# Priority of the first-stage matmuls over x's second half, and a split of the last output stores, in an S4D + gated-GLU kernel

## Chip, core and metric

The kernel runs on one core of a Trainium2 chip. The metric is the device time of one execution in microseconds (us); the median of 3 runs of the kernel before is 713.99 us (711.97 to 716.0). Engines: PE is TensorE, DVE VectorE, ACT ScalarE, POOL GpSimd, SP SyncE.

## What is computed

With `xn` the layer norm of `x` (2048 positions, D = 448 channels), the result is `x + S4D(xn) + GLU(xn)`. The first branch is a long convolution with a kernel generated from 256 complex modes per channel, the second a gated MLP with F = 1792:

```python
# S4D branch: K from exp(A dt pos), then a convolution by FFT
P = jnp.exp((A * dt[:, None])[:, :, None] * pos[None, None, :])
K = 2.0 * jnp.einsum("dn,dnl->dl", C, P).real
y = irfft(rfft(u_t, 2 * L) * rfft(K, 2 * L)[None], 2 * L)[:, :, :L]
y = y + u * D_skip
# GLU branch
h = sigmoid(xn @ w_gate) * (xn @ w_up)
h @ w_down
```

All of it is float32 in accuracy: a float32 operand of the GLU is split into a high and a low part (`hh`/`hl`, `wh`/`wl`, `dh`/`dl`, `xh`/`xl`), and three products of the parts are summed.

## The kernel before

Two Python generators run side by side and hand their instructions to a scheduler: `conv()` for the S4D branch and `glu()` for the MLP. A table of estimated weights decides which generator gets the next turn; the scheduler then orders each engine's instructions by a rank (their place in the program, lowered by `HP` = 300 inside `with hp(HP):`) and by what it holds to be ready. On the chip each engine runs its own list strictly in that order, so an instruction that waits holds up all that stands behind it.

The GLU runs in two halves of 1024 positions. In each half `gate` (L695) multiplies x's transposed blocks by a 128-wide slice of the gate and up weights (L709, 11 matmuls per PSUM bank `gu`), ACT takes the tanh (`th`, L717), DVE multiplies (`hf`, L720), ACT and DVE split the product (`hh` L725, `hl` L727), and the down projection (`po`, L825) adds into `acc` by a DVE instruction (L830). `th`, `hf`, `hh`, `hl`, `acc` all have the raised rank.

The convolution first generates its kernel: per group of 8 channels two matmuls `tr` (L542), four ACT instructions `S` (L548 to L551), POOL products `me` and `mf` (L520), three large DVE products `Et`, `Et`, `Ft` (L602 to L604), and 32 small matmuls `ko` (L616) of 128 rows by 32 columns of PE. Later, in `spectra`, the two spectra are multiplied and turned back (L902, L929, L962), and DVE adds the result to the accumulators (L970).

In the last group of the GLU's first half (`cross`), the second half of x is prepared in four pairs of blocks (8, 10, 12, 14). `pair_norm` normalizes two blocks, `pair_turn` transposes them (L213, with copies L219 to L226), and `pair_first` (L681) does the first stage of their Fourier transform: four groups g, each two matmuls (L280) of 32 rows by 64 columns of PE into one `gu` bank, a copy of that bank to SBUF by ACT (L689) and a store to `x1_d` by ACT's queue (L691). The pool of `gu` banks has four buffers, shared by `gate`, `po`, `pair_turn` and `pair_first`: a matmul into a new bank waits until the bank's last reader is done.

At the end of the program the last group writes the output. `out` (L235) issues four stores, one for each 32 partitions, dealt round a list of queues. `accs[2]` holds blocks 8 to 11, `accs[3]` blocks 12 to 15. The first channel half (0 to 223) of the convolution is added long before the end; the second (224 to 447) is added by the four DVE instructions L970 that stand between the down projections of blocks 14 and 15.

Of the kernel before, what the change touches and what calls it, by code (L numbers as in the profile page):

```python
# [20 lines left out]
D = 448  # L21
# [15 lines left out]
HP = 300  # L37
Y0 = (8, 1)
CP = D // 4
H = D // 2  # L40
# [91 lines left out]
def s4d_glu_kernel(ctx, tc, io):  # L132
    nc = tc.nc
    hp = tc.high_priority
# [56 lines left out]
    def acc_tile():  # L191
        return pg.tile([128, 4, D], F32, name="acc", bufs=2)
# [37 lines left out]
    accs = [acc_tile() for _ in range(2)]  # L230

    def blocks(t, g, b0, nb):
        return t[g, :, b0 // 8, b0 // 4 % 2, b0 % 4 : b0 % 4 + nb]

    def out(src, b0, nb, ds, engs):  # L235

        for g in range(4):
            eng = engs[g % len(engs)]
            eng.dma_start(blocks(out_t, g, b0, nb)[:, :, ds], src[32 * g : 32 * g + 32, b0 % 4 : b0 % 4 + nb, ds])
# [33 lines left out]
    def row(b, g):  # L273
        return 32 * (b // 4 % 2) + 8 * g + 4 * (b // 8) + b % 4

    def x_first_stage(to, xn, g):

        s = slice(32 * g, 32 * g + 32)
        for i in range(2):
            nc.tensor.matmul(to[64 * i : 64 * i + 64], wx[s], xn[i][s], start=True, stop=True)  # L280
# [400 lines left out]
    def pair_first(b, xns):  # L681

        x1 = pg.tile([128, 2, D], F32, name="x1", tag="wraw", bufs=1)
        pss = [psg.tile([128, 512], F32, name="gu", bufs=4) for _ in range(4)]
        for g in range(4):
            x_first_stage(pss[g][:, :D], xns, g)
        for g in range(4):
            to = x1[:, g] if g < 2 else pg.tile([128, D], F32, name="x1", tag="rd", bufs=RB)
            nc.scalar.copy(to, pss[g][:, :D])  # L689
            r = row(b, g)  # L690
            nc.scalar.dma_start(  # L691
                x1_d[:, r : r + 2].rearrange("h i k d -> (i k) h d"), to.rearrange("p (h d) -> p h d", h=2)
            )
# [36 lines left out]
    def glu():  # L730
        for half in range(2):
# [4 lines left out]
            for fs_ in ORDER[half]:  # L736
# [3 lines left out]
                final = half == 1 and fs_ is ORDER[1][-1]  # L740
# [4 lines left out]
                if cross:  # L745
                    xts = {b: pair_load(b) for b in range(8, 16, 2)}
                    step = lambda f_, b: f_(b, xts[b])
                    mid = [(pair_norm, 8), None, (pair_first, 8), (pair_first, 10)]
                    end = [(), ((pair_turn, 8), (pair_norm, 10)), ((pair_turn, 10), (pair_norm, 12)), ((pair_turn, 12), (pair_norm, 14))]
                    downs = {(0, 0): (pair_first, 12), (0, 1): (pair_turn, 14), (0, 3): (pair_first, 14)}  # L750
# [54 lines left out]
                for t in range(2):  # L805
                    acc = accs[2 * half + t]
                    for b in range(4):
                        if final and (t, b) == (0, 1):

                            yield None  # L810
                        if final and t == 1 and b >= 2:

                            sp_mm[:] = glu_mm
                            for m in (4 * b - 8, 4 * b - 6):
                                lasts[0](1, m)
                            if b == 3:
                                out(accs[2], 8, 4, slice(H, D), (nc.sync, nc.scalar))
                                out(accs[3], 12, 3, slice(0, D), (nc.sync, nc.scalar))
                        po = psg.tile([128, D], F32, name="po", tag="gu", bufs=4)
                        bs = slice(128 * b, 128 * b + 128)  # L820
                        n = 0
                        with tc.issue_after(sp_mm[0].ins) if glu_on else nullcontext():
                            for (hh, hl), (dh, dl) in zip(hs[t], wts):
                                for a_, w_ in ((hh, dh), (hh, dl), (hl, dh)):
                                    glu_mm[:] = [nc.tensor.matmul(  # L825
                                        po, a_[:, bs], w_, start=(n == 0), stop=(n == 3 * fc - 1)
                                    )]
                                    n += 1
                        with hp(HP):
                            v.scalar_tensor_tensor(  # L830
                                acc[:, b], po, 0.5, acc[:, b], ALU.mult, ALU.add
                            )
                        yield 0.6 * fc
                        if cross and (t, b) in downs:
                            step(*downs[t, b])
                    if cross:
                        nc.sync.dma_start(acc_d[:, 4 * t : 4 * t + 4], acc)
                    if final and t == 0:
                        out(acc, 8, 4, slice(0, H), (nc.gpsimd,))
                    elif final:  # L840
                        out(acc, 15, 1, slice(0, D), (nc.sync, nc.scalar))

    def spectra(pf):

# [265 lines left out]
    xq, psc, raws, acl, marks, slots, pqs = list(x_first), [], [], [], [None, None], {}, []  # L1110
    W1s, GGs, act, exps = [], [], [], []
    gens = [conv(), glu()]
    total = [sum(Y0) + 11 * WP + 8 * WX + 34 + NCK * WK + HOLE + 17 * WS, 2 * (4 + NFT * 14.8) - HELD]
    done = [0.0, 0.0]
# [40 lines left out]
```

## Time and profile before

| What | Value |
|---|---|
| median of 3 runs | 713.99 us |
| time of the profiled execution | 710.54 us |
| its span, first to last instruction | 708.8 us |
| busy PE / DVE / ACT / POOL | 94% / 78% / 60% / 54% of the span |
| mean granted TensorE clock | 0.988 |

The profiled execution is 3.45 us below the median, inside the spread of the runs. In the views, "idle" in square brackets is the time an engine waited just before the instruction and the name behind the arrow is what ended the wait. A count x8 in the trace's rows of L280 is 4 of the program's matmuls, and x64 of L616 is 32: each of these float32 matmuls leaves two records.

### The profile page before, as it was taken

How to read it: one execution, taken by the hardware profiler on the slowest of the kernel's cores; microseconds unless marked ns; L12 is line 12 of the kernel's file. 1: busy time of each engine (PE TensorE's matmuls, PEld its weight loads, DVE VectorE, ACT ScalarE, POOL GpSimd, SP SyncE). 2: the span in 40 equal slices, each digit the busy share in tenths (PEclk: the TensorE clock that was granted, in tenths of full speed). 3: DMA queues.
4: the chain of work that ended last, by engine and by line, in shares of the span. 5: the costliest groups of instructions: out<-in, count | busy, mean ns of one | idle time of the engine just before them, and what ended most of it. 6: DMA issues, size and time to landing. Idle time of an engine off the chain costs nothing. (4 is left out here: it accounts for less than half of the span.)

```text
span 708.8 us, 19098 instructions
## 1 busy us (share of the span) xinstructions
PE 668.1 (94%) x7752; PEld 523.7 (74%) x7752; DVE 555.7 (78%) x766; ACT 428.7 (60%) x678; POOL 384.9 (54%) x433
## 2 busy tenths in 40 slices
PE   2798999999999998999999999999999999999996
PEld 2575878878877875756878878877777777777784
DVE  5899987699899998898478899988946555566544
ACT  3656965578689779877577788778543322322320
POOL 2101227655999999777446698798765001344001
PEclk9999999999999998989999999999999999999999
DMA  9956274554253544546833333242269988999756
GB/s 200 239 149 204 70 230 150 170 183 132 63 169 135 169 123 135 162 146 202 258 112 103 92 112 108 68 138 82 54 179 280 257 236 238 266 272 221 182 146 182
DMA packets 93031, 117.22 MB, mean 165 GB/s; under 512 B 12240, under 2 KB 76624, under 8 KB 92944
## 3 DMA queue, kind: packets, MB, share of 16 engines
q1 hardware_dynamic: 65376, 91.75, 46.3%
q10 hardware_dynamic: 24896, 18.13, 8.7%
q0 software_dynamic: 2672, 6.13, 3.2%
q8 instruction: 61, 1.00, 0.6%
q14 instruction: 26, 0.21, 0.1%
HBM read 72.13 MB, written 43.84 MB: 164 GB/s over the span
## 5 line engine op out<-in xcount | busy, mean ns | idle before, releaser
L520 POOL TENSOR_TENSOR me<-me,pm 128x32 f32<-128x32 f32 (+1 forms) x168 | 154.9, 922 | 66.8 <-DVE Et L603 38.1
L520 POOL TENSOR_TENSOR mf<-mf,pm 128x64 f32<-128x64 f32 (+1 forms) x112 | 116.9, 1044 | 5.1
L709 PE MATMUL gu<-xh,wh 128*128 128x512 f32 x336 | 100.1, 405 | 3.8 <-DVE acc L830 1.6
L709 PE MATMUL gu<-xh,wl 128*128 128x512 f32 x336 | 96.9, 393 | 0.0
L709 PE MATMUL gu<-xl,wh 128*128 128x512 f32 x336 | 95.1, 390 | 0.0
L602 DVE TENSOR_TENSOR Et<-me,S 128x1024 f32<-128x1024 f32 x56 | 80.2, 1433 | 11.6 <-ACT S L551 10.3
L825 PE MATMUL po<-dh,hh 128*128 128x448 f32 x224 | 84.2, 376 | 3.1 <-ACT hh L725 1.9
L548 ACT ACTIVATE S<-tr 128x1024 f32<-128x1024 f32 x56 | 57.7, 1030 | 44.9 <-PE tr L542 41.0
L604 DVE TENSOR_TENSOR Ft<-mf,S 128x1024 f32<-128x1024 f32 x56 | 80.1, 1431 | 5.3 <-PE ko L616 3.7
L603 DVE TENSOR_TENSOR Et<-me,S 128x1024 f32<-128x1024 f32 x56 | 80.4, 1436 | 4.8 <-ACT me L533 4.5
L825 PE MATMUL po<-dh,hl 128*128 128x448 f32 x224 | 82.4, 369 | 0.3 <-DVE hl L727 0.3
L825 PE MATMUL po<-dl,hh 128*128 128x448 f32 x224 | 82.3, 368 | 0.0
L709 PEld LDWEIGHTS gu<-xh,wh 128*128 128x128 f32 x336 | 60.8, 189 | 24.2 <-issue 4.4
L709 PEld LDWEIGHTS gu<-xh,wl 128*128 128x128 f32 x336 | 63.4, 189 | 14.7 <-DVE ve L255 0.7
L709 PEld LDWEIGHTS gu<-xl,wh 128*128 128x128 f32 x336 | 63.0, 188 | 13.5
L725 ACT CAST hh<-hf 128x512 fp32r<-128x512 f32 x56 | 34.9, 623 | 62.4 <-DVE hf L720 61.4
L616 PEld LDWEIGHTS ko<-Et,Ft 128*32 128x32 f32 x3584 | 54.7, 112 | 24.2 <-issue 13.4
L720 DVE SCALAR_TENSOR_TENSOR hf<-th,gu 128x512 f32<-128x512 f32 x56 | 38.1, 680 | 39.9 <-PE gu L709 35.2
L786 POOL TENSOR_TENSOR dl<-rd,dh 128x448 fp32r<-128x448 f32 x14 | 25.6, 1830 | 78.8 <-ACT dh L785 68.5
L616 PE MATMUL ko<-Et,Ft 128*32 128x64 f32 x3584 | 65.2, 223 | 2.6 <-DVE Ft L604 2.4
L551 ACT ACTIVATE S<-S,hpi 128x1024 f32<-128x1024 f32 x56 | 65.5, 1170 | 0.0
L717 ACT ACTIVATE th<-gu 128x512 f32<-128x512 f32 x56 | 33.5, 599 | 49.4 <-PE gu L709 43.0
(208 smaller groups left out, 1318.0 us busy)
## 6 DMA issues: line engine op xcount, KB each, us to landing
sk_d<-sk ACTq DMA_DIRECT2D x14, 512.0 KB
sx<-x_d SPq DMA_DIRECT2D x32, 224.0 KB
skl<-sk_d SPq DMA_DIRECT2D x16, 448.0 KB
vp<-v_d SPq DMA_DIRECT2D x16, 448.0 KB
v_d<-vt SPq DMA_DIRECT2D x14, 448.0 KB
ph<-ph_d SPq DMA_DIRECT2D x224, 24.0 KB
wt_d<-wh SPq DMA_DIRECT2D x9, 512.0 KB
wt_d<-wl SPq DMA_DIRECT2D x9, 512.0 KB
```

What stands on the lines that cost most here:

```text
L520: ins = nc.gpsimd.tensor_tensor(m[:, :, w + a : 2 * w : n], m[:, :, a:w:n], par(base + i).unsqueeze(2).to_broadcast([128, 4 * DC, w // n]) ...
L548: nc.scalar.activation(rows(cs), pv, AF.Abs)
L551: sins[:] = [nc.scalar.activation(cs, cs, AF.Sin, scale=-TWO_PI, bias=hpi)]
L602: v.tensor_tensor(Et[:, :, :, 32:64], two(me[:, :, 32:64]), S[:, 1::-1], ALU.mult)
L603: v.tensor_tensor(Et[:, :, :, 0:32], two(me[:, :, 0:32]), S[:, 1:3, :, ::-1], ALU.mult)
L604: fts[:] = [v.tensor_tensor(Ft, two(mf), S[:, 3:5], ALU.mult)]
L616: mm = nc.tensor.matmul(ko[32 * j : 32 * j + 32, sl], Ft[:, cc, DC * h + 4 * q + j], Et[:, cc, DC * h + 4 * q + j], start=(k == 0), stop=( ...
L709: glu_mm[:] = [nc.tensor.matmul(ps, a_, b_, start=(n == 0), stop=(n == len(mm) - 1))]
L717: marks[0] = nc.scalar.activation(th, pgu[0], AF.Tanh, scale=0.5)
L720: marks[1] = v.scalar_tensor_tensor(hf, th, 1.0, pgu[1], ALU.add, ALU.mult)
L725: nc.scalar.copy(hh, hf)
L825: glu_mm[:] = [nc.tensor.matmul(po, a_[:, bs], w_, start=(n == 0), stop=(n == 3 * fc - 1))]
```

## The change

Two edits. First, `pair_first` wraps its matmuls (through `x_first_stage`, L276) and ACT's copies in `hp(HP)`, so that both have the rank of the gate's functions; its DMA issues keep theirs. Second, the output stores of blocks 12 to 15 are cut in another way. Before: blocks 12 to 14 whole after the last L970, block 15 whole after its L830. After: of blocks 12 and 13 the first channel half is stored by POOL's queue as soon as block 13's L830 is done, the second half by SP and ACT after L970; blocks 14 and 15 go together, whole, after block 15's L830.

```diff
@@ pair_first
-        for g in range(4):
-            x_first_stage(pss[g][:, :D], xns, g)
+        with hp(HP):
+            for g in range(4):
+                x_first_stage(pss[g][:, :D], xns, g)
         for g in range(4):
             to = x1[:, g] if g < 2 else pg.tile([128, D], F32, name="x1", tag="rd", bufs=RB)
-            nc.scalar.copy(to, pss[g][:, :D])
+            with hp(HP):
+                nc.scalar.copy(to, pss[g][:, :D])
@@ glu, final group, second half of its positions
                                 out(accs[2], 8, 4, slice(H, D), (nc.sync, nc.scalar))
-                                out(accs[3], 12, 3, slice(0, D), (nc.sync, nc.scalar))
+                                out(accs[3], 12, 2, slice(H, D), (nc.sync, nc.scalar))
...
+                        if final and (t, b) == (1, 1):
+                            out(acc, 12, 2, slice(0, H), (nc.gpsimd,))
...
                     elif final:
-                        out(acc, 15, 1, slice(0, D), (nc.sync, nc.scalar))
+                        out(acc, 14, 2, slice(0, D), (nc.sync, nc.scalar))
```

Lines 687 to 816 of the kernel before stand two lower in the changed one, those behind 832 four lower. The instructions outside the stretch of the four pairs and the tail keep their order but for single steps.

**PE, pair 10.** Here `gu<-xt,wx` are `pair_first`'s matmuls (two rows' worth, x2, is one group g), `ko<-Et,Ft` the convolution's small matmuls, `gu<-ident,xt` transposes, `tr` the convolution's phase matmuls. Before:

```order
L709 MATMUL gu<-xl,wh 128x512 x3
L280 MATMUL gu<-xt,wx 64x448 x4
L213 MATMUL gu<-ident,xt 64x128 x2
L542 MATMUL tr<-sel,ph_1111 128x512 x2
L616 MATMUL ko<-Et_1104,Ft 32x64 x32
L280 MATMUL gu<-xt,wx 64x448 x4
L709 MATMUL gu<-xh,wh 128x512 x3
```

The same place on PE in the changed kernel:

```order
L711 MATMUL gu<-xl,wh 128x512 x3
L280 MATMUL gu<-xt,wx 64x448 x2
L616 MATMUL ko<-Et_1104,Ft 32x64 x11
L280 MATMUL gu<-xt,wx 64x448
L213 MATMUL gu<-ident,xt 64x128 x2
L280 MATMUL gu<-xt,wx 64x448
L616 MATMUL ko<-Et_1104,Ft 32x64 x17
L280 MATMUL gu<-xt,wx 64x448 x2
L616 MATMUL ko<-Et_1104,Ft 32x64 x4
L542 MATMUL tr<-sel,ph_1111 128x512 x2
L280 MATMUL gu<-xt,wx 64x448 x2
L711 MATMUL gu<-xh,wh 128x512 x3
```

The eight matmuls stood in two runs of four; now they stand in five runs, two of them of a single matmul, with pieces of one `ko` group between them.

**DVE, pair 12.** The row `hf<-th,gu` is the GLU product that frees the bank for `pair_first`'s first group; `Et`, `Et`, `Ft` are the convolution's large products; `xl` are the splits of the transposed blocks. Before:

```order
L602 TENSOR_TENSOR Et_1104<-me_1109,S_1103 128x32x32
L603 TENSOR_TENSOR Et_1104<-me_1109,S_1103 128x32x32
L720 SCALAR_TENSOR_TENSOR hf<-th,gu 128x512
L269 TENSOR_SCALAR xt<-xt,ys,zs 128x448
L220 TENSOR_TENSOR xl<-gu,xh 128x2x256
L604 TENSOR_TENSOR Ft<-mf_1108,S_1103 128x1024
```

DVE at the same place in the changed kernel:

```order
L722 SCALAR_TENSOR_TENSOR hf<-th,gu 128x512
L269 TENSOR_SCALAR xt<-xt,ys,zs 128x448
L602 TENSOR_TENSOR Et_1104<-me_1109,S_1103 128x32x32
L603 TENSOR_TENSOR Et_1104<-me_1109,S_1103 128x32x32
L729 TENSOR_TENSOR hl<-hf,hh 128x512
L604 TENSOR_TENSOR Ft<-mf_1108,S_1103 128x1024
```

`hf` has moved ahead of two `Et` products, and `xl` (no longer in the six rows) behind `Ft`.

**SP, the last stores.** `ac` holds blocks 0 to 7, `acc` the accumulators of blocks 8 to 15. Before:

```order
L945 DMA v_d<-vt 128x896
L951 DMA vp<-v_d 16x32x224
L239 DMA out_dram<-ac 32x4x224 x4
L239 DMA out_dram<-acc 32x4x224 x2
L239 DMA out_dram<-acc 32x1344 x2
L239 DMA out_dram<-acc 32x448 x2
```

The end of SP's list in the changed kernel:

```order
L949 DMA v_d<-vt 128x896
L955 DMA vp<-v_d 16x32x224
L239 DMA out_dram<-ac 32x4x224 x4
L239 DMA out_dram<-acc 32x2x224 x2
L239 DMA out_dram<-acc 32x4x224 x2
L239 DMA out_dram<-acc 32x896 x2
```

ACT's list ends in the same way. The small stores of blocks 12 and 13 (32x2x224) now stand ahead of those of blocks 8 to 11, and the last ones are twice as large (32x896 for 32x448). POOL's list gains four stores 32x2x224 at its end.

## The prediction

> **What bounds the kernel now.** I read the busy table in stretches of 20 us first, then the same table in stretches of 5 us around the four pairs, PE's waits there, and the timeline. Columns: length, busy time and instruction count of PE, PE's weight loads, DVE, ACT and POOL, then the granted clock, the DMA share, GB/s.
>
> ```profile
> 60.00:80.00 20.00, 17.21 (x83) 14.96 (x84) 19.31 (x38) 17.39 (x38) 0.00 (x0) 1.00 0.50 148
> ...
> 360.00:380.00 20.00, 19.87 (x266) 16.14 (x265) 16.18 (x19) 14.36 (x22) 12.97 (x19) 1.00 0.44 143
> ...
> 460.00:480.00 20.00, 19.76 (x323) 16.00 (x322) 17.51 (x15) 14.88 (x22) 19.69 (x20) 1.00 0.52 155
> ...
> 680.00:700.00 20.00, 20.00 (x223) 16.23 (x219) 10.68 (x21) 1.50 (x3) 2.18 (x4) 1.00 0.54 138
> ```
>
> PE is full from 340 us on: 19.87 and 19.76 of 20 in two stretches of the middle, 20.00 at the end. What delays PE at the pairs should therefore reach the end of the program nearly one to one. The pairs themselves look different:
>
> ```profile
> 275.00:280.00 5.00, 3.75 (x74) 1.53 (x62) 5.00 (x6) 5.00 (x9) 4.92 (x4) 0.93 0.15 49
> 280.00:285.00 5.00, 5.00 (x73) 3.15 (x73) 3.38 (x3) 5.00 (x9) 4.84 (x7) 0.50 0.56 177
> 285.00:290.00 5.00, 5.00 (x79) 3.79 (x77) 2.90 (x5) 3.24 (x6) 3.83 (x6) 0.89 0.47 142
> 290.00:295.00 5.00, 4.97 (x92) 3.43 (x85) 5.00 (x7) 4.85 (x9) 2.12 (x4) 1.00 0.73 225
> 295.00:300.00 5.00, 5.00 (x92) 3.03 (x85) 4.94 (x5) 5.00 (x10) 4.84 (x4) 1.00 0.39 119
> ...
> 305.00:310.00 5.00, 3.27 (x37) 1.26 (x38) 5.00 (x9) 5.00 (x9) 4.60 (x8) 1.00 0.29 101
> 310.00:315.00 5.00, 5.00 (x53) 2.91 (x53) 4.96 (x6) 5.00 (x9) 4.69 (x5) 0.50 0.42 128
> 315.00:320.00 5.00, 5.00 (x71) 3.83 (x70) 4.65 (x6) 3.83 (x7) 0.27 (x2) 0.82 0.27 92
> ...
> sum 75.00, PE 69.61 PEld 46.34 DVE 63.80 ACT 64.66 POOL 59.66; mean PE 4.64 PEld 3.09 DVE 4.25 ACT 4.31 POOL 3.98
> ```
>
> Two things are to be seen. From 265 to 340 us PE is idle 75 - 69.61 = 5.4 us, while DVE has 63.80 of 75 filled, so PE and DVE bound this part by turns. And twice, behind a thin stretch (3.75 and 3.27 of 5), the clock is halved: work lost is (0.07 + 0.50 + 0.11) x 5 = 3.4 us the first time, (0.50 + 0.18) x 5 = 3.4 us the second.
>
> **The first edit: pieces.** What a run of L280 costs PE is in its timeline (start, length, count):
>
> ```profile
> 275.76 0.97 PE L280 MATMUL gu<-xt,wx 32*64 32x448 f32 x4
> 277.98 0.97 PE L280 MATMUL gu<-xt,wx 32*64 32x448 f32 x4 [1.25 <-DVE xl L220]
> 278.88 0.41 PE L213 MATMUL gu<-ident,xt 128*64 128x128 f32 x2
> ...
> 294.60 0.98 PE L280 MATMUL gu<-xt,wx 32*64 32x448 f32 x8
> 295.51 0.41 PE L213 MATMUL gu<-ident,xt 128*64 128x128 f32 x2
> ...
> 305.91 1.99 PE L280 MATMUL gu<-xt,wx 32*64 32x448 f32 x8 [0.92 <-DVE hf L720]
> ...
> 322.36 0.99 PE L280 MATMUL gu<-xt,wx 32*64 32x448 f32 x12
> ...
> 326.18 0.41 PE L213 MATMUL gu<-ident,xt 128*64 128x128 f32 x2 [0.75 <-DVE xl L223]
> ```
>
> Four records (one group g) hold PE for 278.88 - 277.98 = 0.90 us, eight (two groups) for 295.51 - 294.60 = 0.91, twelve for 0.99. The groups lie in different rows of the array and run side by side, but only when they follow each other. The price is per run, not per matmul. Before, the trace has 4 runs in pair 8 (each group by itself), 2 in pair 10, 3 in pair 12 (the row of 1.99 us is two that a wait parts) and 2 in pair 14: 11. The changed order has 5, 5, 3 and 4: 17. Six more runs are 6 x 0.90 = 5.4 us of PE. Four of the runs are single matmuls, for which the trace has no row; between half a run (0.45) and a whole one, I take the whole, since both matmuls of a group already lie side by side in different columns. The lower end is 5.4 - 4 x 0.45 = 3.6 us. Ten cuts of `ko` for seven add a few tenths at most, which I leave out.
>
> What of this shows, pair by pair:
>
> - Pair 8, one run more, and six of the 32 `ko` matmuls moved behind the 1.25 us gap, all just as the clock halves: up to 2 us. But DVE waits behind it now:
>
> ```profile
> DVE hf L720 <- PE gu L709: 2.1, 1, 2.1
> ...
> DVE Ft L604 <- PE ko L616: 1.6, 1, 1.6
> ```
>
> The changed order lets DVE do an `Et` ahead of that `hf`, so the 2.1 us are used and little is left of the delay. I take +0.2, bounds 0 and +2.
> - Pair 10, three runs more: PE has no gap from 290 to 300 us that could take them. +2.7, lower bound 3 x 0.90 - 2 x 0.45 = +1.8.
> - Pair 12, no run more. `hf` ran late because two `Et` stood ahead of it on DVE:
>
> ```profile
> 303.18 2.08 DVE L603 TENSOR_TENSOR Et<-me,S 128x1024 f32<-128x1024 f32 x1
> 305.18 0.67 DVE L720 SCALAR_TENSOR_TENSOR hf<-th,gu 128x512 f32<-128x512 f32 x1
> ```
>
> Now it stands ahead of them and PE's gap of 0.92 us goes: -0.9. Next late is `xl`, which moves behind `Ft` (bound: a new gap of one `Et`, about +2).
> - Pair 14, two runs more, +1.8, with gaps of 0.75 and 0.17 us beside them that can take half: +0.9, bounds 0 and +1.8. Here a down projection comes to wait for DVE's last split of the earlier pair, which stands behind five large products.
>
> Sum +2.9 us. ACT's copies only change places; its queue of small DMA issues is off the path, since x1_d is read much later.
>
> **The clock.** Everything ahead of the first halved stretch is unchanged, so that one stays. The second followed a thin stretch made of L280 runs and two gaps. The changed order fills that place better, but thins out pair 10 (4.5 us of L280 runs in about 6.5 us, each on a quarter of the array or less) and pair 14. I keep the count at two: 0, bounds -3.4 and +6.8. [...]
>
> **The second edit: the tail.**
>
> ```profile
> 694.75 0.62 DVE L830 SCALAR_TENSOR_TENSOR acc<-po,acc 128x448 f32<-128x448 f32 x1 [1.23 <-PE po L825]
> ...
> 699.41 2.21 DVE L970 TENSOR_TENSOR acc<-acc,pv 128x448 f32<-128x448 f32 x4 [0.34 <-PE pv L962]
> 702.12 0.62 DVE L830 SCALAR_TENSOR_TENSOR acc<-po,acc 128x448 f32<-128x448 f32 x1 [0.50 <-PE po L825]
> ```
>
> ```profile
> 703.81 1.79 SPq L239 DMA_DIRECT2D out_dram<-acc  x2
> ```
>
> ```profile
> DMA  9999679977899899999989998894794000000000
> GB/s 315 275 359 287 187 215 343 319 231 203 207 203 191 207 291 347 410 379 362 311 287 311 335 335 263 263 287 128 263 343 136 8 0 0 0 0 0 0 0 0
> DMA packets 1677, 1.93 MB, mean 215 GB/s; under 512 B 287, under 2 KB 1549, under 8 KB 1677
> ```
>
> The last rows cover 700 to 709 us in 40 slices: the DMA engines are nearly full until slice 31, 700 + 31 x 0.225 = 707.0, moving 1.93 MB in 7 us, 276 GB/s. The last data is ready at 702.12 + 0.62 = 702.74, but SP issues its store at 703.81 only: the tail is bound by bytes. The change takes 4 x 56 KB = 0.23 MB out of it, 0.23 / 0.276 = 0.83 us, and has POOL issue them from 694.75 + 0.62 = 695.4 on, into a hole:
>
> ```profile
> DMA  8677596200030000000004988988999999767997
> ```
>
> (694 to 702 us, 0.2 us each: almost nothing from 695.6 to 698.2.) Against it, the last four stores carry 0.46 MB instead of 0.23. If they leave no earlier than now, they end 0.83 us later. They should leave earlier, because what stands ahead of them is smaller and can start with the second L970 instruction. I take -0.6, bounds -0.8 and +0.8.
>
> **Sum.** +2.9 + 0 - 0.6 = +2.3 us: the profiled execution of 710.54 us becomes 712.8, and the median of 713.99 becomes **716.3 us** (+0.3%).
>
> **Rivals.**
>
> - *A further halved stretch.* Pair 10, cut into single runs, falls under what the clock needs, around 300 us, or pair 14 does around 318 us. For it speaks that both halved stretches follow such places; against it that 325 to 330 us was left at 1.00. Price 3.4 us: 716.3 + 3.4 = 719.7, slower. It decides if pair 10's 5 us hold more L280 than other work on PE. Two of them: 723.
> - *One halved stretch less.* `hf` ahead of the `Et` products closes the gaps at 305 and 309 us, the clock stays, and no other place is thin enough: 716.3 - 3.4 = 712.9.
> - *DVE sets the pace.* PE's extra runs lie under DVE's work altogether (63.80 of 75 us), so +2.9 becomes -0.9, and the second halved stretch goes as well: 713.99 - 0.9 - 3.4 - 0.6 = 709.1, faster. Against it speaks pair 10, where PE had no gap.
> - *Only the tail counts*: pieces and gaps cancel, 713.4.
>
> **Chances.** Forecast 0.42; further halved stretch 0.23; one less 0.14; DVE sets the pace 0.15; only the tail 0.06. Faster by over 0.5% (below 710.4, about what a measurement can tell from no change) is the DVE case and a little of its neighbour: 0.18. Slower by over 0.5% (above 717.6) is the further stretch and some 0.4 of the forecast, whose bounds reach 2 us up: 0.39. Within: 0.43. The range leaves out the DVE case's lower half and two further stretches: 710.0 to 721.5.
>
> **What would show it.** In the changed profile: runs of x2 or x4 of L280 at 0.9 us each, 17 of them; PE still full around 295 us, with pair 10's gate matmuls 2 to 3 us later than at 298; no wait of L280 for `hf` in pair 12; two stretches at clock 0.50; DMA at the end done about 4.3 us behind the last L830 + 0.62, now 707.0 - 702.7. Wrong would be: single runs at 0.45 us or less, a third stretch at 0.50 or only one, or a delay at 340 us that is gone at 540.

## The result and the profile after

The change makes the kernel **slower by 0.7%**: 717.25 us median (714.32 to 722.64, 10 runs) against 712.52 us (710.1 to 716.0, 10 runs) of the kernel before on the same chip, ratio 1.0069, 95% interval 1.0043 to 1.0096, so 3.1 to 6.8 us. The predicted 716.3 us lies 0.95 us below, inside the range, but the predicted difference was 2.3 us and the measured one is 4.7. That the times lie so close is in part luck: the 713.99 us from which the forecast started, a median of three runs, stands 1.47 us above the median of ten. The profiled execution of the changed kernel is the fastest of its ten: 714.32 us, span 712.5, mean clock 0.989 (before: 710.54, 708.8, 0.988). Ratios are taken without runs that lie over 1.5% above the fastest of their kernel; for one experiment (`turns_up_tail`) that leaves out three of twelve, and its median stands higher than its ratio says.

Where the time came in, the start of one and the same `hf` product on DVE tells, behind the four pairs and near the end. In the timeline of the changed kernel:

```profile
343.95 0.69 DVE L722 SCALAR_TENSOR_TENSOR hf<-th,gu 128x512 f32<-128x512 f32 x1 [4.46 <-PE gu L711]
...
681.18 0.69 DVE L722 SCALAR_TENSOR_TENSOR hf<-th,gu 128x512 f32<-128x512 f32 x1 [3.05 <-PE gu L711]
```

The same two in the kernel before:

```profile
340.31 0.69 DVE L720 SCALAR_TENSOR_TENSOR hf<-th,gu 128x512 f32<-128x512 f32 x1 [4.41 <-PE gu L709]
...
676.70 0.69 DVE L720 SCALAR_TENSOR_TENSOR hf<-th,gu 128x512 f32<-128x512 f32 x1 [3.05 <-PE gu L709]
```

3.64 us late behind the pairs, 4.48 us at 677 us, and 712.5 - 708.8 = 3.7 at the end: the delay is made at the pairs, grows a little, and the tail gives 0.8 back. Now pair 8 on PE in the changed kernel (start, length, idle time ahead):

```profile
273.66 0.97 PE L280 MATMUL gu<-xt,wx 32*64 32x448 f32 x4 [0.76 <-DVE hf L722]
...
275.12 0.97 PE L280 MATMUL gu<-xt,wx 32*64 32x448 f32 x4
...
277.81 1.75 PE L280 MATMUL gu<-xt,wx 32*64 32x448 f32 x2 [1.16 <-DVE xl L220]
279.49 0.64 PE L213 MATMUL gu<-ident,xt 128*64 128x128 f32 x2
280.06 1.75 PE L280 MATMUL gu<-xt,wx 32*64 32x448 f32 x2
...
283.46 1.76 PE L280 MATMUL gu<-xt,wx 32*64 32x448 f32 x4
285.15 1.94 PE L616 MATMUL ko<-Et,Ft 128*32 128x64 f32 x64
```

Five runs, three of them at half clock at 1.7 us each (285.15 - 283.46). And pair 10, at full clock:

```profile
296.85 0.97 PE L280 MATMUL gu<-xt,wx 32*64 32x448 f32 x4
297.75 0.54 PE L616 MATMUL ko<-Et,Ft 128*32 128x64 f32 x22
298.22 0.96 PE L280 MATMUL gu<-xt,wx 32*64 32x448 f32 x2
299.11 0.41 PE L213 MATMUL gu<-ident,xt 128*64 128x128 f32 x2
299.44 0.96 PE L280 MATMUL gu<-xt,wx 32*64 32x448 f32 x2
300.34 0.75 PE L616 MATMUL ko<-Et,Ft 128*32 128x64 f32 x34
```

A single matmul (x2 records) holds PE for 299.11 - 298.22 = 0.89 us, a group of two for 297.75 - 296.85 = 0.90. There are 17 runs in all. The stretches of 5 us, columns as in the prediction:

```profile
275.00:280.00 5.00, 3.84 (x44) 1.16 (x35) 3.68 (x5) 5.00 (x9) 4.91 (x5) 0.76 0.15 51
280.00:285.00 5.00, 5.00 (x21) 1.48 (x20) 2.36 (x2) 2.94 (x6) 2.04 (x5) 0.50 0.16 54
285.00:290.00 5.00, 5.00 (x77) 4.00 (x75) 2.73 (x3) 3.90 (x5) 4.92 (x7) 0.72 0.54 173
...
310.00:315.00 5.00, 4.79 (x69) 2.55 (x71) 5.00 (x8) 5.00 (x8) 4.75 (x8) 1.00 0.42 145
...
320.00:325.00 5.00, 2.91 (x49) 2.46 (x48) 4.94 (x8) 4.57 (x7) 2.19 (x6) 1.00 0.14 49
```

Through the pairs the clock is halved in one stretch of 10.24 us (lost: (0.24 + 0.50 + 0.28) x 5 = 5.1 us) where before had two of 6.83 us, which lost 3.4 us each, and 320 to 325 us, the thinnest place, keeps 1.00.

To put all kernels on one scale I summed PE's timeline from the `hf` at 263.94 us of before to the tenth `hf` behind it, at 404.73: each row holds PE from its start to the next row's start less that row's idle time; half of what lies at clock 0.50 goes to "clock", the rest to its kind of work. Differences from before in us; the last but one column is the mean over all runs of time x granted clock, that is the time less what the clock took (a halved stretch in which PE idles anyway is counted there too).

| Kernel | stretch | L280 | turns L213 | ko L616 | other PE work | PE idle | clock | time x clock, all runs | ratio (95%) |
|---|---|---|---|---|---|---|---|---|---|
| before | 140.8 | 10.1 | 4.0 | 20.4 | 93.8 | 5.6 | 6.8 | 701.6 | |
| changed | +3.9 | +5.0 | +0.6 | +0.6 | 0.0 | -0.5 | -1.8 | +4.6 | 1.0069 (1.0043 to 1.0096) |
| rank_only | +6.9 | +5.0 | +0.6 | +0.8 | 0.0 | -0.9 | +1.4 | +4.8 | 1.0090 (1.0060 to 1.0121) |
| rank_mm | +6.2 | +5.0 | +0.6 | +0.7 | -0.3 | -0.9 | +1.2 | +4.9 | 1.0059 (1.0036 to 1.0081) |
| tail_only | -1.5 | +0.1 | 0.0 | +0.2 | +0.4 | +1.2 | -3.4 | +0.6 | 1.0006 (0.9976 to 1.0036) |
| up400 | +5.2 | +3.4 | +0.4 | +1.0 | +0.6 | +0.4 | -0.6 | +3.9 | 1.0052 (1.0027 to 1.0078) |
| rank_in8 | +4.6 | +1.0 | +0.2 | +0.4 | -0.1 | +3.2 | 0.0 | +2.9 | 1.0061 (1.0038 to 1.0084) |
| rank_in10 | +4.9 | +3.6 | -0.1 | -0.2 | -0.4 | +2.0 | 0.0 | +4.1 | 1.0047 (1.0022 to 1.0072) |
| rank_in1012 | +6.1 | +4.2 | -0.4 | +0.2 | -0.4 | -0.9 | +3.4 | +2.0 | 1.0054 (1.0032 to 1.0077) |
| in12_tail | +4.6 | +1.9 | +0.1 | +0.1 | +0.3 | +0.7 | +1.5 | +1.7 | 1.0042 (1.0015 to 1.0069) |
| t_1214 | +4.2 | -0.9 | -0.4 | -0.6 | +0.8 | +1.8 | +3.5 | -0.3 | 1.0040 (1.0014 to 1.0065) |
| turns_up_tail | +10.2 | -1.3 | -0.3 | 0.0 | +0.3 | +7.2 | +4.2 | +3.0 | 1.0061 (1.0028 to 1.0093) |
| ko_nohp | +9.9 | -2.8 | +0.1 | -0.2 | -0.5 | +9.1 | +4.2 | +4.0 | 1.0124 (1.0090 to 1.0158) |
| ko_hp | +13.6 | -1.1 | 0.0 | +0.6 | +0.5 | +8.9 | +4.7 | +6.9 | 1.0192 (1.0158 to 1.0226) |

The granted clock of a run is given to three places, which is 0.7 us; the columns of PE are one execution each.

### The profile page after: what moved, and what is told of

Its sections match the earlier page's. It is cut to its first block, busy times and chain, and to the rows that moved or that the text cites. A ratio compares the mean times of both kernels' runs of the same rounds, so it can differ in the third digit from the quotient of the medians.

```text
span 712.5 us, 19088 instructions
## 1 busy us (share of the span) xinstructions
PE 674.7 (95%) x7752; PEld 525.4 (74%) x7752; DVE 556.3 (78%) x766; ACT 428.9 (60%) x678; POOL 384.8 (54%) x437
## 4 chain that ended last, share of the span: by engine, by line
PE 66%; DVE 15%; POOL 6%; ACT 4%; issue 3%; DMA 3%; SPq 2%; DVEq 0%; ACTq 0%; POOLq 0%
PE gu L711 29%; PE po L827 12%; PE sp L906 7%; PE ko L616 5%; PE pv L933 4%; POOL me L520 3%; PE tr L542 3%; DVE Et L603 2%; DVE Ft L604 2%; POOL mf L520 2%; PE gu L280 2%; DVE Et L602 2%; DMA acc<-in_A_u_dram 1%; PE pv L966 1%; PE kp L566 1%
## 5 line engine op out<-in xcount | busy, mean ns | idle before, releaser
L520 POOL TENSOR_TENSOR me<-me,pm 128x32 f32<-128x32 f32 (+1 forms) x168 | 149.8, 891 | 68.9 <-DVE Et L603 40.0
L604 DVE TENSOR_TENSOR Ft<-mf,S 128x1024 f32<-128x1024 f32 x56 | 82.5, 1473 | 10.7 <-PE ko L616 9.3
L616 PEld LDWEIGHTS ko<-Et,Ft 128*32 128x32 f32 x3584 | 54.7, 111 | 29.3 <-issue 17.0
L711 PEld LDWEIGHTS gu<-xl,wh 128*128 128x128 f32 x336 | 63.5, 189 | 13.6
L616 PE MATMUL ko<-Et,Ft 128*32 128x64 f32 x3584 | 65.7, 223 | 3.9 <-DVE Ft L604 3.6
```

The source lines that it names most:

```text
L520: ins = nc.gpsimd.tensor_tensor(m[:, :, w + a : 2 * w : n], m[:, :, a:w:n], par(base + i).unsqueeze(2).to_broadcast([128, 4 * DC, w // n]) ...
L604: fts[:] = [v.tensor_tensor(Ft, two(mf), S[:, 3:5], ALU.mult)]
L616: mm = nc.tensor.matmul(ko[32 * j : 32 * j + 32, sl], Ft[:, cc, DC * h + 4 * q + j], Et[:, cc, DC * h + 4 * q + j], start=(k == 0), stop=( ...
L711: glu_mm[:] = [nc.tensor.matmul(ps, a_, b_, start=(n == 0), stop=(n == len(mm) - 1))]
```

## The experiments

The leading theory is that of the pieces: each run of L280 costs PE 0.9 us whatever it holds, the raised rank makes 17 runs of 11, and that is the slowdown. Rivals: ACT's raised copies, the tail, the clock alone, and PE's waits for DVE.

**The two edits apart.** `rank_only` has the first edit alone, `tail_only` the second.

> The first edit alone: matmuls and copies of the first stage have the raised rank, the stores at the end are cut as before. Theory of the pieces: PE's order holds 17 runs of L280 for 11, so PE leaves the pairs about 3.8 us late, and the kernel is slower by 4.5 to 6.5 us (ratio 1.006 to 1.009), a little more than the whole change, whose tail gives back 0.8. Theory of the clock: what counts is where the halved stretches fall; this profile then shows another sum of halved time than before's 13.7 us, and the delay at 340 us differs from 3.6 by the difference. Theory of the tail: nearly nothing, within 0.2% of before.

> The second edit alone: the stores of blocks 12 to 15 cut as in the change, PE's order through the pairs as before. Theory of the pieces: -0.8 us, ratio 0.998 to 1.000, and the marks through 340 us as before within 0.3 us unless a halved stretch falls elsewhere. If the tail were what costs: slower by 3 us or more. The profile is also a second look at before's order of the pairs: if the clock's stretches alone made the difference between before and after, their place here should differ from before's and the delay at 340 us with it.

`rank_only` 719.34 us median, ratio 1.0090; `tail_only` 712.80, 1.0006. All of the slowdown that can be told apart comes with the first edit, at the upper end of what was expected; the tail alone came out just above its 0.998 to 1.000, with an interval that reaches into it. As to the first edit, the time x clock of all runs puts it at +4.8 us with the clock left out. PE's order in `rank_only` is that of the changed kernel; its stretch of the table is 3.0 us longer, and its clock took 3.2 us more. So the clock moves single executions by some us, but both have the +5.0 us of L280. The tail's own worth is too small for the times, but not for the profiles: from the last `hf` to the end of the span it takes 32.0 to 32.2 us in the nine profiles with the old stores and 31.2 to 31.6 in the five with the new ones, so the tail gains 0.4 to 1.0 us. In the timeline of the changed kernel POOL's four early stores stand at 700.15, as soon as block 13 is done:

```profile
699.23 0.62 DVE L832 SCALAR_TENSOR_TENSOR acc<-po,acc 128x448 f32<-128x448 f32 x1 [1.23 <-PE po L827]
700.15 2.15 POOL L239 DMA_DIRECT2D out_dram<-acc  x4 [1.53 <-DVE acc L832]
...
706.61 0.62 DVE L832 SCALAR_TENSOR_TENSOR acc<-po,acc 128x448 f32<-128x448 f32 x1 [0.50 <-PE po L827]
```

**Copies or matmuls.** `rank_mm` raises the matmuls alone (cut shown against the first edit).

```diff
         with hp(HP):
             for g in range(4):
                 x_first_stage(pss[g][:, :D], xns, g)
...
-            with hp(HP):
-                nc.scalar.copy(to, pss[g][:, :D])
+            nc.scalar.copy(to, pss[g][:, :D])
```

> The first edit for the matmuls alone: ACT's copies keep their old rank, the tail is as before, PE's list is that of the whole change (17 runs of L280). Theory of the pieces: as with matmuls and copies, slower by 4 to 8 us (ratio 1.006 to 1.011). Theory of the copies (raised copies hold up the gate's tanh and squares on ACT): at most 1.003.

The ratio is 1.0059, just under the 1.006 to 1.011 expected and with an interval that overlaps that of `rank_only`; L280 takes the same +5.0 us, and time x clock is +4.9 us for +4.8. So the copies' rank adds nothing that shows, and that rival is ruled out.

**Fewer runs by waiting.** `ko_hp` and `ko_nohp` place a pair's matmuls behind the last `ko` group issued so far, with the raised and the old rank (cut of `ko_hp`; in `ko_nohp` `hp(HP)` is left out).

```diff
+                ko_mm[:] = [mm]
...
+        with hp(HP), tc.issue_after(ko_mm[0].ins):
             for g in range(4):
                 x_first_stage(pss[g][:, :D], xns, g)
```

> Raised rank for matmuls and copies as in the first edit, but the matmuls of a pair are released only behind the last group of the convolution's small matmuls that the program has issued by then, so that they stand in 10 runs for 17 (before: 11). Theory of the pieces: the cost of the first edit goes; the delay at 340 us is within 1.5 us of before's, ratio 0.998 to 1.003. Theory of the rank (functions of the GLU come later whatever the runs are): still slower by 4 us or more. Tail as before.

> Rank as before, and the matmuls of a pair released as in the run above: 8 runs of L280 for before's 11. Theory of the pieces: three runs less are 2.7 us of PE, so 1 to 3 us faster than before (ratio 0.996 to 0.999) unless DVE's splits, which then come later, take them. Theory of the clock: no gain unless a halved stretch goes; then 3.4 us a stretch. Tail as before.

My expectation failed by far: 725.94 us (1.0192) and 721.26 (1.0124). The runs of L280 did what was said: the 8 of `ko_nohp` take 7.2 us, the 10 of `ko_hp` 8.9. But PE's timeline of `ko_hp` in pair 8 shows what was paid for it:

```profile
274.06 1.10 PE L616 MATMUL ko<-Et,Ft 128*32 128x64 f32 x64
279.11 0.64 PE L213 MATMUL gu<-ident,xt 128*64 128x128 f32 x2 [3.95 <-DVE xl L223]
...
281.80 1.93 PE L616 MATMUL ko<-Et,Ft 128*32 128x64 f32 x64 [1.20 <-DVE Ft L604]
...
287.14 1.93 PE L616 MATMUL ko<-Et,Ft 128*32 128x64 f32 x64 [1.55 <-DVE Et L602]
289.00 1.80 PE L280 MATMUL gu<-xt,wx 32*64 32x448 f32 x16
```

All eight matmuls are one run, of 1.8 us at half clock, and PE stood idle for 7 us in pieces ahead of it: with the matmuls gone from the front there is nothing to do while DVE finishes, and the clock falls on top (4.2 to 4.7 us more than before). So a theory that the time follows the number of runs alone is wrong.

**One pair at a time.** `rank_in8`, `rank_in10` and `rank_in1012` raise the rank of matmuls and copies in the pairs named, here pair 8.

```diff
+        up = (lambda: hp(HP)) if b in (8,) else nullcontext
+        with up():
             for g in range(4):
                 x_first_stage(pss[g][:, :D], xns, g)
```

> Raised rank in pair 8 alone. The list has 12 runs of L280 (5, 2, 3, 2) for 9 of before (3, 2, 2, 2), where waits make 11 of the 9. Theory of the pieces: PE spends 0.9 us for each further run, 2 to 3 us in all, and at the end 1.5 to 3 us are left (ratio 1.002 to 1.004) beside what the clock does. Theory that only waits count: PE's time in L280 may grow, but the time at the end follows PE's idle time through the pairs, not the runs.

> Raised rank in pair 10 alone: 13 runs in the list (3, 4, 3, 3) for 9, none of a single matmul. Theory of the pieces: 3 to 4 further runs, 2.7 to 3.6 us of PE, ratio 1.003 to 1.006. Theory that only waits count: as for pair 8 alone.

> Raised rank in pairs 10 and 12: 15 runs in the list (3, 4, 4, 4) for 9. Theory of the pieces: 4 to 6 further runs as executed, 3.6 to 5.4 us of PE, ratio 1.005 to 1.009; over before, pair 10 alone, this one and the whole first edit, the time without the clock's loss rises by about 0.9 us a run. Theory that only waits count: no such line.

The ratios are 1.0061, 1.0047 and 1.0054; the first lies above the 1.002 to 1.004 expected, the others inside. In pairs 10 and 10 with 12, L280 grows by 3.6 and 4.2 us as foreseen. With pair 8 alone it grows by 1.0 us only, where 2 to 3 were expected, and the rest is idle time, 3.2 us more. Two waits that before did not have come to more than that together, while smaller ones went (in `rank_in8`'s timeline of PE):

```profile
304.81 0.94 PE L712 MATMUL gu<-xh,wh 128*128 128x512 f32 x3 [1.81 <-DVE xr L226]
...
320.07 0.67 PE L616 MATMUL ko<-Et,Ft 128*32 128x64 f32 x32 [2.42 <-DVE Et L602]
```

The line of 0.9 us a run over these kernels isn't there: +4.1 us of time x clock for pair 10 alone, +2.0 for two pairs. The price of a run is the same each time (0.89 to 0.91 us for the 14 at clock 1.00 in the changed kernel, 0.89 to 0.97 in twelve of the fourteen rows of L280 in `rank_in10`'s timeline); what a reordering does to PE's idle time is of the size of a few runs and differs from order to order (+3.2, +2.0 and -0.9 us in these three).

**Whole groups.** `up400` raises the matmuls' rank by 400, the copies' by 300 as in the change, and in the program's order no group is parted (cut shown against the first edit).

```diff
-        with hp(HP):
+        with hp(400):
             for g in range(4):
                 x_first_stage(pss[g][:, :D], xns, g)
```

> First edit with a rank raised by 400 in place of 300, tail as before: the matmuls of a group are never parted any more, 14 runs of L280 in the list (4, 4, 4, 2) for the 17 of the change. Theory of the pieces: PE's time in L280 falls by 2.7 us against the first edit alone (15.1 to about 12.5 us), and the kernel is 2 to 4 us faster than that one, 1.002 to 1.006 of before. Theory of the rank (any raise costs the same): as the first edit alone, 1.008 to 1.010.

L280 falls by 1.7 us against `rank_only` (13.4 for 15.1; 2.7 was expected, since waits part one more run), the ratio is 1.0052 for 1.0090, and time x clock 0.9 us lower. That goes the way of the pieces, but the two intervals overlap, and against `rank_mm` (1.0059), which has the order of `rank_only`, the ratio is hardly lower. So this run supports the price of a piece by its L280, not by its time.

**Held until the transposes.** `turns_up_tail` is the whole change with a pair's matmuls issued behind the last transpose issued so far (first line below, in place of the change's `with hp(HP):`); `t_1214` does so at the old rank, for pairs 12 and 14 alone, with the new tail (second line).

```diff
+        with hp(HP), tc.issue_after(turns[0].ins):
...
+        with tc.issue_after(turns[0].ins) if b > 10 else nullcontext():
```

> Both edits of the change, with the raised matmuls of a pair held until the pair's last transpose has been issued: 10 runs of L280 (2, 3, 2, 3) for 17. Theory of the pieces: L280 takes about 9 us, and if PE's idle time through the pairs stays within 2 us of before's 5.6, the time is within 0.3% of before. But the transpose of pair 8 now stands behind a whole group of the convolution's matmuls, as in the two kernels held behind that group, and there PE waited 7 us for DVE's split: if that wait returns, slower by 8 us or more. Which of the two, the profile's idle time tells.

> Old rank, new tail, and only the matmuls of pairs 12 and 14 held until the transposes: 9 runs in the list (3, 2, 2, 2), the convolution's groups cut into 9 parts for 13, pairs 8 and 10 with before's order. An attempt at a faster one: L280 9 to 10 us, idle time as before within 1.5 us, clock as it falls, tail 0.5 to 0.8 us shorter, so 0.996 to 1.001 of before. If PE's waits for DVE grow as in the held kernels: 1.003 or more.

The times are 719.19 us (1.0061) and 715.75 (1.0040). In the first, the wait of pair 8 came back: 4.21 us for `xl` ahead of the transpose at 278.12 us, and 7.2 us more idle time in all; the slowdown lies between the two that had been expected. The second shows the trade most plainly: less work in L280, turns and `ko` (-1.9 us), yet more idle time and a clock that stays down, in its stretches of 5 us:

```profile
305.00:310.00 5.00, 2.34 (x28) 1.49 (x30) 5.00 (x6) 4.60 (x8) 4.61 (x7) 0.86 0.48 163
310.00:315.00 5.00, 5.00 (x72) 2.37 (x63) 5.00 (x8) 4.69 (x9) 4.75 (x5) 0.50 0.11 27
315.00:320.00 5.00, 2.71 (x39) 1.32 (x38) 4.90 (x6) 2.94 (x6) 1.09 (x2) 0.50 0.28 93
320.00:325.00 5.00, 5.00 (x34) 3.65 (x33) 1.52 (x4) 3.25 (x6) 3.32 (x6) 0.50 0.27 91
```

Without the clock's loss its runs are as fast as before's (-0.3 us, within their scatter); with it they are slower, by the 1.003 or more that had been expected if PE's waits grow. I had hoped that this one would beat both kernels.

**Two single runs.** `in12_tail` has both edits, the rank raised in pair 12 alone (the cut shows the matmuls; the copies follow the same condition).

```diff
+        up = (lambda: hp(HP)) if b in (12,) else nullcontext
+        with up():
```

Ahead of pair 12 PE's list is that of before, and behind it chiefly `ko` groups, transposes and phase matmuls change places.

> Both edits, but the rank is raised in pair 12 alone: PE's list ahead of pair 12 is that of before, pair 12 has 4 runs of L280 (4, 1, 1, 2 matmuls) for 2 in the list, pair 14 two as before, so 11 for 9. Theory of the pieces: L280 takes 0.9 to 1.8 us more than before's 10.1 from pair 8 to pair 14, the tail is 0.5 to 0.8 us shorter, and the time is 1.000 to 1.003 of before. Theory that the waits decide: the transposes of pair 14 now start ahead of the convolution's group, PE's idle time there falls by more than the runs cost, and this one beats both kernels, under 0.998.

The time is 716.08 us, the ratio 1.0042, above the 1.000 to 1.003 expected. Its pair 12 on PE:

```profile
310.37 1.75 PE L280 MATMUL gu<-xt,wx 32*64 32x448 f32 x2 [0.54 <-DVE acc L833]
312.05 0.63 PE L213 MATMUL gu<-ident,xt 128*64 128x128 f32 x2
312.62 1.75 PE L280 MATMUL gu<-xt,wx 32*64 32x448 f32 x2
...
315.09 1.76 PE L280 MATMUL gu<-xt,wx 32*64 32x448 f32 x4
```

Two further runs cost 1.93 us of work in L280, 0.96 each, and here they fall into a halved stretch and so hold PE for 1.7 us each. Of the 4.6 us by which its stretch is longer, the clock has 1.5 and idle time 0.7. This is the cleanest case of a piece and its price; none of these kernels beats the kernel before.

## Why the prediction was right, and where it was not

**The pieces: right in mechanism and price.** 17 runs for 11 were counted and are there; 0.90 us was assumed also for a single matmul, and 0.89 is measured, so the lower end, 0.45, is ruled out. Six more runs were to cost 5.4 us of PE, and L280 takes 5.0 us more. The few tenths left out for the cuts of `ko`, and transposes parted in the same way, measure 0.6 and 0.6 us.

**The cover: wrong, the step that failed.** The prediction let 2.5 of the 5.4 us vanish in gaps and behind DVE (+2.9 shown). PE's idle time fell by 0.5 us only (0.9 in `rank_only`, whose order is the same). Pair 8 was taken at +0.2, because DVE's wait of 2.1 us for the gate would be used. That wait is gone, but by the first L280 of pair 10 PE is 2.25 us late (296.85 for 294.60), 2.4 us more than at the start of pair 8 (273.66 for 273.83). In place of that wait DVE got others, as its timeline in the changed kernel shows:

```profile
282.43 1.23 DVE L604 TENSOR_TENSOR Ft<-mf,S 128x1024 f32<-128x1024 f32 x1 [3.74 <-PE ko L616]
...
287.21 1.66 DVE L604 TENSOR_TENSOR Ft<-mf,S 128x1024 f32<-128x1024 f32 x1 [2.42 <-PE ko L616]
```

PE was full, with runs at half clock, and DVE waited for the `ko` behind them. Of the 2.4 us, 1.6 are the clock's, since the halved stretch there is half as long again; 0.7 are L280 and 0.4 `ko`, and PE idles only 0.1 us less there than before. Pair 10, +2.7, measured +3.2 (gate at 303.72 for 298.26: 5.46 late, where 2 to 3 had been named, less 2.25). Pair 12, -0.9, measured -2.0 (the down projection behind it at 316.76 for 313.31); the wait for `hf` is gone as predicted, but 1.7 us of the gain are the clock's: before had its second halved stretch there, which the changed profile has not. Pair 14 came out near nothing between that projection and the `hf` at 344 us (3.45 to 3.64 late) for +0.9, but again because before lost 1.8 us to that stretch there. L280 takes 1.7 us more, and the idle time that was to take half of it grew by 1.0. Its foretold wait is there, a down projection that waits for `xr` behind five large products on DVE:

```profile
323.16 0.47 PE L827 MATMUL po<-dh,hh 128*128 128x448 f32 x1 [2.09 <-DVE xr L226]
```

and waits of before (0.75 and others) went for it only in part. The sum of the pairs is +3.8 (3.64 and the 0.17 that the changed profile was ahead). With the clock's loss taken out as in the table, the four pairs come to +0.8, +3.2, -0.4 and +2.0, or +5.6 for the +2.9 predicted: of 6.2 us of added work (5.0 + 0.6 + 0.6) about half a us was covered.

**The clock: right in size, wrong in form.** Two stretches were to stay; the changed profile has one, half as long again (10.24 us for 6.83), which the prediction had named as a sign of being wrong. The profiles of `rank_only` and `rank_mm`, with PE in the same order through the pairs, have two, of 13.65 and 3.41 us. Over all runs the loss is 11.3 us before and 11.7 after, so the term of 0 holds for the kernel, while single runs differ by far more. The changed kernel's ten runs have mean clocks from 0.976 to 0.989: the rival of a further stretch is what some of them are, and not others; what the clock needs to stay at 1.00, no run shows.

**The tail: right**, -0.6 for a measured -0.8. The sign named for it, DMA done 4.3 us behind the last product, contradicted the term: with the term of -0.6 it had to be 3.7. In the changed kernel's DMA view from 704 us on (40 slices of 0.2125 us) the engines are nearly full up to 704 + 32 x 0.2125 = 710.8 us, 3.6 us behind 706.61 + 0.62:

```profile
DMA  9998888999999997778988999999987400000000
```

**One to one to the end: nearly.** 3.64 us became 4.48 by 677 us, so a little was added on the way.

In sum: predicted +2.9 + 0 - 0.6; in the profile +4.5 - 0.8 = +3.7, with a clock that took 1.8 us less through the pairs; in the medians +4.7. The chances gave most to "within 0.5%", by the cover; with the bare price of the pieces, 5.4 less 0.6, the forecast would have been slower by 0.7%, which is what was measured.

What stays open: why one order makes PE's idle time grow by 3 us and another shrinks it by 1, which I can read off but could not have foreseen from the order; and what begins a halved stretch.

## What to carry to other kernels

The small matmuls here, of 32 rows by 64 columns, paid by the run and not by the matmul: 0.89 us for one, 0.90 for two, 0.91 for four. Count how often other work parts such matmuls, and price each part in full, a single matmul too. Where two engines bound a stage by turns, as PE and DVE did here, don't subtract an engine's wait from the other's added work unless the row that ends that wait stays where it is; add the work in full and let the cover be the lower bound: of 6.2 us added here, about half a us was covered. And joining pieces by holding them back bought nothing in four kernels here (ratios 1.0040 to 1.0192, PE's idle time up by 1.8 to 9.1 us), because the piece was what the engine did while it waited.

## What the runs showed of the hardware

The halved stretches in the traces' clock records have lengths of 3.41, 6.83, 10.24, 13.65 and 17.07 us, all multiples of 3.41 (the last of a trace, which the end of the record cuts, left out): 6.83 twice in the kernel before, 3.41 and 10.24 in the changed one, 13.65 and 3.41 in `rank_only`, 17.07 in `t_1214`. In the changed kernel, `rank_only` and `rank_mm`, whose PE order through the pairs is the same, the first one there begins at 277.6, 278.7 and 276.2 us, that is 13.8, 13.4 and 12.5 us behind the `hf` with which the table's stretch begins: with one order of PE the start differs by up to 1.3 us. The length of an idle gap did not tell here where a stretch begins: the one of 10.24 us began in the changed kernel at 277.6 us, in a gap of 1.16 us with one of 0.76 us ahead of it, while the gap of 2.09 us ahead of 323.16 us left the clock at 1.00, as did 2.8 us of idle in all between 60 and 80 us in the kernel before.

A good part of the runs' spread goes with the clock. The nine runs of `turns_up_tail` that its ratio uses reach from 714.45 us at a mean clock of 0.986 to 721.36 at 0.978, and a fit over them gives 0.85 us of time for each us lost. Over 90 runs of the kernel before it is about 0.75, with much scatter. An explanation that would fit is that a stretch costs less where PE waits anyway. `tail_only` shows such a case: its profile lost 3.4 us less to the clock than before's, had 1.2 us more idle time in its place and left the pairs 1.5 us earlier.
